# The second DFT stage of k*v by halves of the channels, in threes of frequencies

## The chip, the cores and the metric

The kernel runs on one core of one Trainium2 chip. The metric is the device time of one execution in microseconds. Five engines work side by side, each with its own queue, in order: TensorE (PE, with its weight loads PEld), VectorE (DVE), ScalarE (ACT), GpSimd (POOL) and SyncE (SP), whose queue issues most transfers. TensorE writes its results to PSUM; ScalarE or VectorE copies ("evicts") them to SBUF.

## What is computed

One block with two parts, over x = A_q of 2048 positions and 640 channels, in bf16, with six modulation vectors made of a condition c. What matters here, cut from the reference:

```python
mod = (_silu(c) @ w_mod).reshape(c.shape[0], 6, 1, -1)       # sa, ca, ga, sb, cb, gb
h = _layernorm(x) * (1 + ca) + sa
# part A: short convolution of k (4 taps) times v, then a long convolution over all positions
kv = k_shift * v
kv_f = rfft(pad(kv), over positions); kf_f = rfft(pad(ssm_k))
y = irfft(kv_f * kf_f)[:S] + kv * ssm_D
x = x + ga * (h * y)
# part B: two gelu MLPs with layer norms, the first with shifts between four channel groups
h = _layernorm(x) * (1 + cb) + sb
h1 = _gelu(_layernorm(h) @ w1); hs = shifted(h1) @ w2; x1 = h + hs
x = x + gb * (x1 + _gelu(_layernorm(x1) @ w3) @ w4)
```

## The kernel before, in words

**The long convolution** is a DFT of 4096 points split into two factors, done with matmuls. Channels lie on partitions in 5 blocks (`ND`); `to_slots` (L392) transposes 32 x 32 pieces on VectorE. `stage1` (L400) multiplies by a small DFT matrix, per channel block b and half h of the channels, and its evictions fill `T01`: the half h = 0 goes to `T0`, h = 1 to `T1`. `stage2` (L417) goes over the 32 frequencies k: for each it does four matmuls (two row halves of the array, g, times two terms, cc), each over the 320 columns of both halves of the channels, into one PSUM slot, and one eviction of 640 elements per partition (`evac`, L206: ScalarE at L209, VectorE at L211). It is called twice: for ssm_k into `KSX` (region R3), and for k*v into `XS` (region R5).

The inverse starts with `inverse1` (L603), ten times, i = 5 h + b. Step i reads block i of `XS`, 2048 columns that hold all 32 frequencies of a tenth of the channels: VectorE multiplies it by the spectrum `kx` and by a copy `ky` of the spectrum with the partition halves swapped (L613, two products per step, into a ring of two pairs `TAB` in Rb). The copy comes by two transfers (L609, one on SP's queue and one on POOL's) into a ring of four buffers `KSY`, which are pieces of RG, RK and Rb: the piece of RK also holds a modulation weight and the small table `Ht`, the piece of Rb the last block of k*v. TensorE then does 2 x 16 matmuls (L624, L625), and two evictions of 1024 elements go to `Zh[h]`, which is `T0` or `T1` again. `inverse2` (L653, matmuls at L665) ends the convolution in groups of two or three position tiles.

**Around it.** `mods` makes the modulation vectors in twelve halves: a weight load from w_mod on SP (L484), five matmuls (L490), an eviction into `modv`. `ln1_stats` and `make_q` make the first normalisation and modulation of each position tile A. `chain_a`, `chain_b`, `chain_c` gate, add, normalise and transpose each tile; `mm_w1`, `mm_w2`, `mm_w3`, `mm_w4` (matmuls L822 and L832, L877, L911, L941) are part B. w3 and w4 are loaded into `T01` once `inverse2` has read all of it.

**What sets the order.** The functions only add tasks to a `Planner`, with dependencies between the regions that they read and write, and with costs and rates that some search outside the kernel used. `run` (L122) takes the order written out in `ORDER`: a number for the task, a letter for its engine (P TensorE, A ScalarE, D VectorE, G POOL, S SP), and after a colon the PSUM slots, of which there are four of two banks each. Each engine executes its tasks in that order. Costs, rates and `port` are not read by `run`.

Of the kernel before, what the change touches and what calls it, by code (L numbers as in the profile page):

```python
# [15 lines left out]
S, D, F = 2048, 640, 1728  # L16
# [10 lines left out]
19G 18D 2S 27G 21G 20D 29D 30A 50G 23D 28D 31A 22D 25A 36G 24A 37G 0S 68G 26G 69D 90P:0 91A 86P:1 84P:2 87A 4S 85A 72G 52D 3S 70G 73D 106P:3 107A 6S  # L27
49G 102P:0 104P:1 105A 71D 96P:2 97A 88P:3 103D 5S 74D 75D 8S 118P:0 98P:1 9S 119D 1S 66D 38G 39G 40A 89A 99A 114P:2 115D 108P:3 92P:0 93A 109A 116P:1
10S 112P:2 94P:0 122P:3 67D 32G 41G 42G 43G 51D 44A 45D 117D 54A 53A 95A 113A 80P:0 81A 11S 123D 110P:1 111D 76P:2 77A 7S 100P:3 101D 82P:0 83A 78P:1
136D 34S 33G 120P:2 121D 46G 55G 79A 179P:3 180A 47S 185P:0 186A 35S 141P:1 142A 191P:3 192D 147P:0 148A 201S 143P:2 144D 175P:1 176A 171P:3 172D  # L30
137P:0 138A 183P:2 184A 195P:1 196D 145P:3 146A 169P:0 170D 48S 163P:2 164A 149P:1 193P:3 194A 197P:0 150D 198D 161P:2 162A 12S 56G 173P:1 174A 204S
189P:3 190D 57G 58G 157P:0 153P:2 154D 151P:1 202S 177P:3 158A 178D 59G 152A 165P:0 166A 139P:2 140D 203S 13S 155P:1 156A 187P:3 188D 159P:0 160A
181P:2 182A 60A 254D 14S 167P:1 168D 199P:3 200D 260P:0 261A 124P:2 212A 268P:0 269A 266P:1 267A 211D 126P:3 125D 127D 262P:0 214D 209A 270P:2 271A
263A 128P:1 264P:3 265A 130P:2 215A 255D 276P:0 15S 129D 61G 210D 65G 258P:3 259A 277A 62G 16S 134P:1 280P:3 281A 131D 63G 17S 135D 363G 278P:2 279A
64A 274P:0 275A 132P:1 213G 272P:3 273A 362S 220S 221P:2 222A 256D 288P:0 289A 133D 257D 282P:1 223S 224P:3 225A 226S 286P:2 287D 283A 284P:0 285D
229S 292P:3 293A 232S 294P:1 295A 290P:2 291D 296P:3 297A 227P:0 228D 387G 230P:1 348P:2 322P:3 239S 231D 480A 235S 349A 340P:0 341A 233P:1 251G 323D
242S 250G 234D 326P:2 360P:3 361D 327A 356P:0 357A 328P:1 329D 241S 358P:2 359A 306P:3 336P:0 337D 307A 314P:1 315A 318P:2 319D 248S 238G 354P:3 355A
320P:0 321D 310P:1 311A 483D 300P:2 252S 330P:3 244S 331D 301A 352P:0 353A 236P:1 253G 237D 308P:2 309A 205S 245G 316P:3 317D 324P:0 325A 350P:1 351D
312P:2 313A 249G 247S 332P:3 333A 243S 246G 298P:0 299D 304P:1 305A 344P:2 345D 302P:3 303A 386S 240G 371G 338P:0 342P:1 343A 339D 334P:2 346P:3 347A
370S 335D 364D 365D 368P:0 369A 366P:1 367A 378S 481D 379G 372D 373D 374P:2 375A 376P:3 377A 486D 487D 380D 381D 442S 443P:0 388D 389D 394S 382P:1  # L40
383A 384P:2 396D 385A 217A 395G 392P:3 397D 402S 403G 390P:1 404D 405D 410S 391A 398P:2 393A 411G 400P:1 412D 399A 408P:3 418S 409A 406P:2 407A 401A
413D 414P:3 415A 416P:2 419G 421D 417A 420D 424P:1 422P:3 425A 423A 448S 449P:2 489A 427G 426S 428D 450A 429D 430P:1 431A 432P:3 434S 435G 437D 433A
436D 438P:2 439A 440P:1 441A 454S 490D 457S 444D 458P:0 479G 445S 455P:3 484D 485D 491D 488D 495P:21 218D 459A 482D 451S 216G 456A 492D 493D 496D 494D
497A 519D 452P:0 453A 446P:3 447D 219G 501G 520D 522G 540D 521A 560D 541D 475S 511P:12 524D 561D 472S 478G 513A 532A 533D 553D 523G 498P:03 499A 500A
591D 588D 525D 534D 527D 592D 542A 589D 512A 543G 545D 544G 563G 565D 502P:20 504A 562A 564G 526A 477S 528G 529D 503A 594D 566D 590A 546D 505P:31 476S
507A 593A 595G 530P:0 531A 567A 568D 547A 548D 651D 600D 601D 508P:21 509A 506A 596D 510A 535P:0 536A 549G 550D 602D 603A 551P:2 206S 569G 570D 597D
537P:3 538A 552D 598D 599A 652D 604D 605G 571P:1 208S 572D 554D 555D 558P:0 559A 606D 609D 473S 654D 655D 556P:2 557A 578P:3 579A 474S 576P:1 577A
610P:0 611D 207S 464D 607P:2 608D 514S 653A 657G 656A 658G 580P:3 581D 582A 620P:1 621A 659D 618P:0 619A 663D 664D 583G 584G 665D 585D 660D 666A
586P:2 625P:3 661D 662A 518G 587A 636P:1 637A 515S 638P:0 639A 622P:2 667D 668G 669D 640P:1 463A 670S 626D 627A 671D 672S 681P:3 517S 679P:0 623D 624A
628D 629G 633D 682A 630D 573D 641A 634P:2 635D 460D 631P:3 642P:1 632D 574D 680A 683P:2 684D 686P:0 687D 643A 575D 703P:1 461A 699P:3 719D 720D 465G  # L50
462G 615D 467A 612D 613D 616D 704A 697P:2 688A 689G 614D 685A 690G 691D 692P:0 700A 694A 695P:1 721A 693D 701P:3 702A 696D 769P:0 765P:1 516S 698A
617D 785D 786D 787A 722D 723D 644P:3 725G 673D 674D 675D 788D 789D 724A 790A 726G 727D 731A 763P:2 770A 791G 466D 728D 729D 730A 645D 792G 705P:03
764A 767P:2 706P 732D 733D 734A 468G 766A 735D 736G 793D 794D 797D 798D 799D 800A 795D 796A 741D 739D 707D 740S 737A 738S 749P:1 750A 747P:0 801G 802G
646D 648S 748A 803D 805D 804S 806S 815P:1 816A 676D 677D 678D 713D 714D 851D 852D 853A 742D 743D 708D 710S 712S 813P:3 711S 754P:0 751P:1 814A 817P:3
709S 854D 855D 856A 755D 752D 768A 771P:02 820P:1 857G 858G 859A 647S 860D 861D 863D 864D 715S 757G 772P 865D 867D 756A 753A 758G 761D 862A 762S 818D
821D 823D 866A 759A 760S 835P:3 819A 822A 868G 869A 824G 827A 871D 773D 470A 872S 836A 825D 779D 780D 829P:1 870S 875P:0 650S 828S 876A 469A 471G 807D
744D 873P:2 745D 826S 895P:3 833P:0 874A 877P:2 896A 808D 809D 834A 914D 880P:3 716S 891P:0 878D 830A 881D 882A 915D 649S 774D 892A 879A 893P:1 831P:2
889P:3 810A 811D 781S 812D 883G 884G 885A 887D 832A 837P:02 894A 886S 888S 955P:1 717S 746D 911D 912D 890A 913A 971D 972D 916A 917G 918G 839D 923D
953P:3 919D 920D 921D 778S 777S 924D 718S 925D 927D 974G 973A 975G 976A 977D 978D 980G 922A 926A 928G 838P 954A 845D 956A 979A 775S 929D 930S 840D
949P:0 897P:23 931A 932S 935P:1 936A 981G 898P 982D 950A 983S 986P:1 987A 783S 539G 841S 933P:0 984P:1 842S 899D 776S 846D 850S 782S 847S 905D 934A  # L60
940P:2 937P:3 941D 985A 848S 938D 844S 784S 900D 989P:0 843S 906D 907S 988G 1023P:1 1024D 951P:2 943G 1026D 992P:3 904S 942A 939A 944G 945D 952A 947D
948S 957P:12 901S 990D 991A 946S 1007P:0 1025A 1027G 993D 1003P:3 994A 995D 996G 997D 1028A 1029S 959D 910S 1008A 999A 998S 1004A 1058P:1 1001P:0
1002A 1005P:3 1000S 1036P:0 1006A 958P 1037A 1032P:3 1033A 1034P:0 1035A 1030P:3 1031A 849S 965D 1062D 960D 961S 908S 903S 902S 966D 969S 1009P:20
964S 1052P:3 909S 1010P 1053A 1011D 1054P:2 1012D 1015S 1055A 1017D 962S 1038P:30 1016S 967S 963S 1018D 970S 1022S 1020S 1021S 1056P:2 1057A 968S
1040D 1041D 1042S 1045S 1043S 1014S 1039P 1046D 1013S 1047D 1044S 1019S 1049S 1050S 1063D 1059A 1051S 1060P:32 1061P 1064D 1065D 1068S 1069S 1066S
1048S 1070D 1071D 1067S 1072S 1074S 1073A 1075A
# [72 lines left out]
def kernel(  # L139
# [294 lines left out]

    def dep(t, *on):
        for o in on:
            if o not in t.deps:
                t.deps.add(o)
                o.succ.append(t)
# [42 lines left out]
    def mod_half(i, j, hf):  # L482
        w, wk = wm[i % 3] if i < EARLY else wl[i - EARLY]
        dma("SP", 410, lambda q: q.dma_start(w, mod_d[:, :, j * D + 320 * hf:j * D + 320 * hf + 320]), w=[wk], rate=250.0)  # L484
# [96 lines left out]
    stage2(XS, "R5")  # L581
# [21 lines left out]
    def inverse1(h, b):  # L603
# [4 lines left out]
        for o in range(2):  # L608
            dma("SP" if o == 0 else "POOL", 256, lambda q, o=o: q.dma_start(ky[64 * o:64 * o + 64, :], kx[64 - 64 * o:128 - 64 * o, :]), r=[kxk], w=[kk + ("y",)], rate=235.0)  # L609
# [90 lines left out]
    def ln_finish(li, t0, n, quick):  # L700
# [4 lines left out]
        def f(e):  # L705
# [3 lines left out]
            else:  # L709
                eng_of[e].tensor_tensor(rs, nm, nm, ALU.mult)  # L710
                eng_of[e].tensor_scalar(rs, rs, -1.0, EPS, ALU.mult, ALU.add)
        add(("POOL", "DVE"), {"POOL": 0.33 * (1 + n), "DVE": 0.15 + 0.12 * n}, f, r=[("s1", 100 * li + t0, 100 * li + t0 + n)], w=[("nm" + k, 0, 1)])

        def f(e):
            if n == 1:
# [353 lines left out]
```

## Time and profile before

| what | value |
|---|---|
| median of 4 runs | 307.48 us (306.92 to 307.85) |
| profiled execution, whole | 307.59 us |
| its span, first to last instruction | 305.8 us |
| busy PE, DVE, ACT, POOL | 272.7, 222.4, 207.2, 112.4 us |
| mean granted TensorE clock | 0.957 |
| first and last L426 matmul of the second call of `stage2` | 62.1 and 74.3 us |
| first L613 product, last L613 product (starts) | 75.36 and 98.22 us |
| first L665 matmul | 102.8 us |
| first L911 matmul | 141.24 us |
| last L932 matmul | 300.20 us |

In the rows of the profile L12 is line 12 of the kernel before. A row of a group gives the line, engine and operation, output<-input by the program's names, partitions x elements, the number of instructions, and then busy us, mean ns of one, and idle time of the engine just before, with what ended it. A row in order of time gives start, duration, engine, line, and in brackets the idle time before it. A row of stretches gives the busy us of each engine between two times. Instructions that follow each other on one engine overlap a little, so that n of them in a row take less than n means. POOL in the chain and DMA rows are transfers by name of their buffers.

### The profile page before, as it was taken

The numbers are of one execution on the slowest core, as the hardware profiler recorded it, in microseconds if no ns is written. First come the engines' busy times: TensorE is split into PE (matmuls) and PEld (weight loads), VectorE is DVE, ScalarE is ACT, GpSimd is POOL, SyncE is SP. The second block draws the span as 40 slices with busy tenths as digits, with TensorE's granted clock in tenths as the row PEclk, the third lists the DMA queues.
The fourth block names the chain that finished last, engine by engine and source line by source line (L and its number), as shares of the span: only waits on it lengthen the run. The fifth ranks groups of instructions, "written<-read, shape, count | busy, mean of one in ns | idle before, by whom it ended". The sixth has DMA issues, their size and how long they took to land.

```text
span 305.8 us, 7408 instructions
## 1 busy us (share of the span) xinstructions
PE 272.7 (89%) x2922; PEld 207.3 (68%) x2926; DVE 222.4 (73%) x437; ACT 207.2 (68%) x355; POOL 112.4 (37%) x257
## 2 busy tenths in 40 slices
PE   0998999997899946697999999999999999999993
PEld 0655655754888724686788777688877777987761
DVE  8999999999999998885688996835755355031343
ACT  4779999998589669986986648875854535522110
POOL 4798066051122786342454722312434042000000
PEclk9999999999799965789999999999999999999998
DMA  5999999779799950961100041250112213201112
GB/s 170 258 204 203 208 198 248 207 197 241 201 230 299 265 104 7 356 212 25 42 3 1 2 91 32 46 107 2 34 37 44 61 29 73 58 11 29 47 39 52
DMA packets 58146, 35.73 MB, mean 117 GB/s; under 512 B 39872, under 2 KB 54848, under 8 KB 58112
## 3 DMA queue, kind: packets, MB, share of 16 engines
q1 hardware_dynamic: 56864, 31.68, 43.2%
q0 software_dynamic: 1152, 3.54, 4.5%
q8 instruction: 23, 0.38, 0.5%
q14 instruction: 11, 0.09, 0.1%
q10 hardware_dynamic: 96, 0.04, 0.1%
HBM read 16.31 MB, written 2.62 MB: 62 GB/s over the span
## 4 chain that ended last, share of the span: by engine, by line
PE 56%; ACT 15%; DVE 10%; DMA 7%; issue 5%; POOL 5%; SPq 0%; ACTq 0%; DVEq 0%; POOLq 0%
PE ps_w L911 20%; PE ps_w L941 19%; PE ps_w L877 6%; ACT T L209 4%; DVE Rb L613 4%; ACT R L209 4%; PE ps_w L822 3%; DMA Ra<-in_A_ssm_k_dram 2%; ACT RG L733 2%; PE ps_s L426 2%; DMA RK<-R 2%; ACT Rb L209 2%; PE ps_s L409 1%; DMA Rb<-R 1%; POOL R L310 1%
## 5 line engine op out<-in xcount | busy, mean ns | idle before, releaser
L911 PE MATMUL ps_w<-R,T 128*128 128x256 bf16 (+1 forms) x630 | 64.3, 261 | 1.0 <-ACT R L782 1.0
L911 PEld LDWEIGHTS <-T 128*128 128x128 bf16 x630 | 55.7, 98 | 8.7 <-issue 2.6
L941 PE MATMUL ps_w<-T,R 128*128 128x320 bf16 x416 | 59.1, 299 | 0.0
L915 ACT ACTIVATE R<-ps_w 128x1024 bf16<-128x1024 f32 (+2 forms) x36 | 29.4, 831 | 36.2 <-PE ps_w L911 30.3
L941 PEld LDWEIGHTS <-R 128*128 128x128 bf16 x416 | 40.5, 98 | 15.2
L964 DVE TENSOR_TENSOR T<-ps_w,R 128x640 bf16<-128x640 f32 x15 | 12.3, 823 | 32.0 <-PE ps_w L941 18.8
L209 ACT CAST T<-ps_s 128x1024 bf16<-128x1024 f32 x33 | 31.4, 1018 | 3.0 <-PE ps_s L409 3.0
L409 PE MATMUL ps_s<-F1bd,Rb 128*128 128x256 bf16 x160 | 22.6, 293 | 9.5 <-DVE Rb L396 8.3
L733 ACT ACTIVATE RG<-R 128x640 bf16<-128x640 bf16 x32 | 23.5, 734 | 10.0 <-DVE R L884 6.5
L409 PEld LDWEIGHTS <-Rb 128*128 128x128 bf16 x160 | 16.6, 105 | 15.6 <-DVE Rb L396 8.3
L209 ACT CAST R<-ps_s 128x640 bf16<-128x640 f32 x37 | 23.4, 721 | 1.2 <-PE ps_s L426 1.2
L624 PE MATMUL ps_i<-EA,Rb 128*128 128x128 bf16 x160 | 20.8, 229 | 2.8 <-DVE Rb L613 2.4
L877 PE MATMUL ps_w<-RG,R 128*128 128x320 bf16 x160 | 23.2, 299 | 0.0
L209 ACT CAST T<-ps_i 128x1024 bf16<-128x1024 f32 x20 | 19.0, 1025 | 5.9 <-PE ps_i L625 5.8
L426 PE MATMUL ps_s<-T,RG 64*128 64x320 bf16 x256 | 22.2, 297 | 0.5 <-DMA RG<-RG 0.2
L625 PE MATMUL ps_i<-EB,Rb 128*128 128x128 bf16 x160 | 20.6, 229 | 1.6 <-DVE Rb L613 1.5
L822 PE MATMUL ps_w<-R,RG 128*128 128x256 bf16 (+1 forms) x200 | 21.8, 276 | 0.0
L719 POOL TENSOR_TENSOR lnv<-lnv,mhalf 128x2 f32<-128x2 f32 (+1 forms) x29 | 20.9, 720 | 2.3
L211 DVE CAST R<-ps_s 128x640 bf16<-128x640 f32 x27 | 20.7, 818 | 0.9 <-PE ps_s L426 0.3
L838 ACT ACTIVATE R<-ps_w1x 32x256 bf16<-32x256 f32 (+1 forms) x40 | 13.2, 331 | 10.6 <-PE ps_w1x L832 10.2
L822 PEld LDWEIGHTS <-RG 128*128 128x128 bf16 x200 | 19.0, 111 | 1.6 <-issue 0.2
L884 DVE SCALAR_TENSOR_TENSOR R<-ps_w,R 128x640 bf16<-128x640 f32 x16 | 13.1, 821 | 9.0 <-PE ps_w L877 9.0
(176 smaller groups left out, 510.0 us busy)
## 6 DMA issues: line engine op xcount, KB each, us to landing
Ra<-in_A_ssm_k_dram SPq DMA_DIRECT2D x5, 512.0 KB, 6.5
Ra<-in_A_q_dram SPq DMA_DIRECT2D x8, 320.0 KB, 6.1
R<-in_w_mod_dram SPq DMA_DIRECT2D x6, 400.0 KB, 7.3
out_dram<-RH SPq DMA_DIRECT2D x60, 40.0 KB, 1.6
T<-in_B_w_dram SPq DMA_DIRECT2D x1, 2160.0 KB, 9.6
T<-in_B_w_dram SPq DMA_DIRECT2D x1, 2080.0 KB, 14.7
RH<-in_w_mod_dram SPq DMA_DIRECT2D x4, 400.0 KB, 5.0
RK<-R SPq DMA_DIRECT2D x5, 256.0 KB, 4.8
```

The source lines that it names most:

```text
L209: nc.scalar.copy(dst, src(ps.tile))
L211: nc.vector.tensor_copy(dst, src(ps.tile))
L409: nc.tensor.matmul(psv[:, ml, :], lhsT=xL[:, s0:s0 + P], rhs=F1r, start=True, stop=True)
L426: nc.tensor.matmul(psv[:, g], lhsT=Gs[p, k, 64 - 64 * cc:192 - 64 * cc], rhs=T1b[p, cc * 32 + k], start=(cc == 0), stop=(cc == 1), tile_po ...
L624: nc.tensor.matmul(psv[:, w, :], lhsT=Av[:, r_, :, g_], rhs=EAf, start=True, stop=False)
L719: nc.gpsimd.tensor_tensor(rs, rs, mhalf[:, 0:n], ALU.pow)
L733: add("ACT", 0.74, lambda e: nc.scalar.activation(junk, src, ACT.Square, scale=float(D) ** -0.5, accum_out=stat[:, li, 1, t:t + 1]), r=[sk ...
L822: nc.tensor.matmul(pt[:, fb, 0:cw], lhsT=w1_sb[:, b, 160 * fb:160 * fb + P], rhs=hT[:, b, 0:cw], start=(b == 0), stop=(b == ND - 1))
L877: nc.tensor.matmul(pt[:, hf, 0:320], lhsT=gsf[:, fb, c0:c0 + P], rhs=w2_sb[:, fb, 320 * hf:320 * hf + 320], start=(fb == 0), stop=(fb == 4))
L911: nc.tensor.matmul(pt[:, fl, 0:cw], lhsT=w3_sb[:, b, fb * P:(fb + 1) * P], rhs=xT[:, b, 0:cw], start=(b == 0), stop=(b == ND - 1))
L915: nc.scalar.activation(g3[g % 2][:, f0:f0 + fn, 0:cw], ps.tile[:, 0:fn, 0:cw], ACT.Gelu_apprx_tanh)
L941: nc.tensor.matmul(bank(i, hf), lhsT=gg[:, fb, i * P:(i + 1) * P], rhs=w4_sb[:, fb, 320 * hf:320 * hf + 320], start=(fb == 0 and i == 0), ...
```

## The change

`stage2(XS, "R5")` is replaced by two calls of a new function, one per half of the channels. Each goes over the frequencies in threes (ten of three and one of two): per group 24 (or 16) matmuls of 160 columns, and one eviction of 960 (or 640) elements. A half reads its half of `T01` and writes its half of `XS`. The first call of `stage2`, for ssm_k, stays. The order is written anew from the first word to the last, so that tasks also change place and engine elsewhere; numbers of tasks from 298 on are shifted. Some costs and rates differ. The whole program has 256 more rows on TensorE (128 weight loads and 128 matmuls), 12 fewer on VectorE, 3 more on ScalarE, 6 fewer on POOL, as many on SP.

```diff
+    def stage2_half(h):
+        for k0 in range(0, 32, 3):
+            kn = min(3, 32 - k0)
+            ps = Slot()
+
+            def f(e, ps=ps, k0=k0, kn=kn):
+                psv = pst(ps, name="ps_s2")[:, :, 0:480].rearrange("p g (k s) -> p g k s", k=3)
+                for j in range(kn):
+                    k = k0 + j
+                    for cc in range(2):
+                        for g in range(2):
+                            p = slice(64 * g, 64 * g + 64)
+                            nc.tensor.matmul(psv[:, g, j], lhsT=Gs[p, k, 64 - 64 * cc:192 - 64 * cc], rhs=T1h[h][p, cc * 32 + k],
+                                             start=(cc == 0), stop=(cc == 1), tile_position=(64 * g, 0))
+            t0 = add("PE", 0.17 * kn, f, r=[("T01", 10240 * h, 10240 * h + 10240), ("RG", 192 * k0, 192 * (k0 + kn))], alloc=ps, ni=8 * kn)
+            w = [("R5", 10240 * h, 10240 * h + 10240, "s2"), ("kT", 4 * h, 5, "s2")] + ([("vT", 0, 5, "s2")] if h else [("kTp", 0, 1, "s2")])
+            t1 = evac(XS[:, 160 * h:160 * h + 160, k0:k0 + kn, :],
+                      lambda t, kn=kn: t[:, :, 0:480].rearrange("p g (k s) -> p s k g", k=3)[:, :, 0:kn], 320 * kn, ps, w)
+            dep(t1, t0)
...
-    stage2(XS, "R5")
+    for h in range(2):
+        stage2_half(h)
...
-        dma("SP", 410, lambda q: q.dma_start(w, mod_d[:, :, j * D + 320 * hf:j * D + 320 * hf + 320]), w=[wk], rate=250.0)
+        dma("SP", 410, lambda q: q.dma_start(w, mod_d[:, :, j * D + 320 * hf:j * D + 320 * hf + 320]), w=[wk], rate=340.0)
...
-        add("POOL", 1.1 if quick else 1.5, f, r=[("s2", 100 * li + t0, 100 * li + t0 + n), ("nm" + k, 0, 1)], w=[("ln" + k, 0, 1)])
+        add("POOL", 0.8 if quick else 1.1, f, port=-1, r=[("s2", 100 * li + t0, 100 * li + t0 + n), ("nm" + k, 0, 1)], w=[("ln" + k, 0, 1)])
```

What the new order does, by engine:

| | before | after |
|---|---|---|
| evictions of the k*v second stage, ScalarE | 19 of 640 | 15 of 960, 1 of 640 |
| the same, VectorE | 13 of 640 | 5 of 960, 1 of 640 |
| evictions of the ssm_k second stage, ScalarE and VectorE | 18 and 14 | 20 and 12 |
| evictions of stage 1 for ssm_k, ScalarE and VectorE | 16 and 4 | 17 and 3 |
| evictions of `inverse1`, ScalarE and VectorE | 20 and 0 | 19 and 1 |
| `ln1_stats`, ScalarE and VectorE | 9 and 7 | 7 and 9 |

On VectorE the last eviction of the first half is followed by one multiplication of q, three products, the one eviction of the second half that VectorE does, and the other seventeen products in a row. On ScalarE six evictions of the second half come first, then the other four between the evictions of `inverse1`. One stage-1 eviction of k*v (its matmuls too) stands within the first half. Of the modulation weights, the sine on ScalarE that frees RK for the third load comes before six more stage-1 evictions of k*v than it did; on SP the load of w1 comes before five of the last six w_mod loads. The last group of `inverse2` comes behind the first three matmul groups of `mm_w1`. Of the first 30 us: the addition of ssm_D for channel block 4 goes from VectorE to POOL, behind the mask of `RQ` (L357), and the sign flip of the first `Gs` block (L350) stays on POOL, but behind the rounding steps of the second.

```diff
-229S 292P:3 293A 232S 294P:1 295A 290P:2 291D 296P:3 297A 227P:0 228D 387G 230P:1 348P:2 322P:3 239S 231D 480A 235S 349A 340P:0 341A 233P:1 251G 323D
-242S 250G 234D 326P:2 360P:3 361D 327A 356P:0 357A 328P:1 329D 241S 358P:2 359A 306P:3 336P:0 337D 307A 314P:1 315A 318P:2 319D 248S 238G 354P:3 355A
...
+290P:0 291A 469D 288P:1 289A 233P:3 234D 292P:2 293A 294P:0 296P:3 230P:1 297A 298P:2 295D 299A 466D 342S 253G 246S 248G 312P:0 308P:3 309A 231D 463D
+300P:1 301A 313D 460D 251G 310P:2 311D 367G 243S 306P:0 307A 316P:3 317D 280P:1 281A 252G 314P:2 304P:0 302P:3 305A 249S 240G 315D 236P:1 303A 237D
+318P:2 319D 467D 340P:0 345D 241S 341A 338P:1 339A 238S 242G 326P:3 327A 344D 245S 250G 366S 322P:2 334P:0 352D 330P:1 331D 323A 244G 335A 239G 247G
...
```

## The prediction

> **What bounds the kernel now.** I read the busy time of each engine by stretches first, then VectorE's and ScalarE's instructions in order of time, then the groups, then the chain. The stretches (busy us, count of instructions; granted TensorE clock, DMA share, GB/s at the end):
>
> ```profile
> core 0: us, PE busy (x) PEld busy (x) DVE busy (x) ACT busy (x) POOL busy (x), PEclk, DMA share, GB/s
> 62.00:75.40 13.40, 12.49 (x140) 7.18 (x138) 12.03 (x19) 12.78 (x20) 5.00 (x10) 1.00 0.94 228
> 75.40:103.00 27.60, 24.06 (x369) 21.72 (x373) 27.50 (x33) 21.70 (x28) 8.25 (x16) 0.94 0.92 253
> 103.00:141.20 38.20, 25.99 (x672) 20.50 (x652) 33.19 (x88) 31.32 (x68) 21.33 (x53) 0.73 0.54 159
> 141.20:160.00 18.80, 18.25 (x200) 15.71 (x200) 12.86 (x34) 15.72 (x34) 8.25 (x22) 1.00 0.13 27
> 160.00:200.00 40.00, 39.61 (x320) 30.06 (x319) 33.93 (x85) 27.21 (x52) 16.96 (x45) 1.00 0.17 36
> 200.00:300.50 100.50, 100.43 (x872) 79.18 (x870) 42.89 (x95) 45.37 (x80) 18.07 (x57) 1.00 0.20 44
> ```
>
> From 141.2 to 300.5 TensorE idles 1.0 us of 159.3: it sets the time there, and an earlier start of that stretch is an earlier end. Before it, from 75.4 to 103, VectorE is busy 27.5 of 27.6 us: the products of the inverse transform. ScalarE is not:
>
> ```profile
> 70.52 4.66 DVE L211 CAST R<-ps_s 128x640 bf16<-128x640 f32 x6 [0.16 <-PE ps_s L426]
> 75.36 1.23 DVE L613 TENSOR_TENSOR Rb<-R,R 128x2048 bf16<-128x2048 bf16 x1 [0.18 <-ACT R L209]
> ...
> 98.22 1.22 DVE L613 TENSOR_TENSOR Rb<-R,R 128x2048 bf16<-128x2048 bf16 x1
> ```
>
> ```profile
> 70.25 5.08 ACT L209 CAST R<-ps_s 128x640 bf16<-128x640 f32 x8 [0.22 <-PE ps_s L426]
> 79.47 1.01 ACT L209 CAST T<-ps_i 128x1024 bf16<-128x1024 f32 x1 [4.15 <-PE ps_i L625]
> ...
> 91.47 6.53 ACT L209 CAST T<-ps_i 128x1024 bf16<-128x1024 f32 x7 [0.52 <-PE ps_i L625]
> ```
>
> Both engines evict the second stage until 75.3; no product can start before the last eviction; then ScalarE waits 4.15 us while VectorE makes the first products. The sizes that I work with:
>
> ```profile
> L426 PE MATMUL ps_s<-T,RG 64*128 64x320 bf16 x256 | 22.2, 297 | 0.5 <-DMA RG<-RG 0.2 <-ACT R L209 0.2
> L209 ACT CAST R<-ps_s 128x640 bf16<-128x640 f32 x37 | 23.4, 721 | 1.2 <-PE ps_s L426 1.2
> L211 DVE CAST R<-ps_s 128x640 bf16<-128x640 f32 x27 | 20.7, 818 | 0.9 <-PE ps_s L426 0.3
> L209 ACT CAST Rb<-ps_i 128x960 bf16<-128x960 f32 x7 | 6.5, 953 | 2.8 <-PE ps_i L665 2.8
> ```
>
> The chain of waits passes through one copy of the kernel's spectrum that comes late, and ends in the stretch of TensorE:
>
> ```profile
> 69.86 6.29 DMA RK<-R
> ...
> 141.24 2.39 PE ps_w L911 x40
> ```
>
> **The evictions.** In a row one costs less than its mean, because neighbours overlap: 5.08/8 = 0.635 us on ScalarE and 4.66/6 = 0.777 on VectorE for 640 elements, 6.53/7 = 0.933 on ScalarE for 1024. For 960 I take 0.88 on ScalarE (0.635 plus the difference of the means, 953 - 721, gives 0.87; on the line to 1024 it is 0.88) and 1.11 on VectorE (the 1024 form has a mean of 1219 against 818; 320/384 of that on top of 0.777). Before: 19 on ScalarE and 13 on VectorE, 12.1 + 10.1 = 22.2 us. After: ScalarE has 15 of three frequencies and one of two, 15 x 0.88 + 0.64 = 13.8; VectorE five and one, 5 x 1.11 + 0.78 = 6.3. VectorE loses 3.8 us, ScalarE gains 1.7. That the access pattern gets one more dimension I cost at nothing: the 960 form of the later inverse step has as many, and fits the line.
>
> **The matmuls.** 128 of 320 columns become 256 of 160, with as many more weight loads. In the trace the four of one frequency start at 65.62, 65.64, 65.75 and 65.77: two row halves of the array run side by side, 0.135 us per pair of 320 columns. Pairs of 160 columns at half of that: 64 half-frequencies x 2 pairs x 0.068 = 8.7 us. If the pairs did not overlap at all, the inverse products give the other end: their 128-column matmuls, each with its own weights, start 0.055 apart (85.17, 85.23, 85.28), so 160 columns cost 0.069 and 256 of them 17.7 us. The Trainium skill has a rule against this change (TensorE: Matmul & The Clock Gate, section Back-to-back issue gap): in a stream of weight loads and matmuls the spacing is about 81 ns at 128 columns and 131 at 512, so short matmuls lose; by it 160 columns are an estimated 0.085 and the stage 21.8 us. The trace has 0.055 where the rule has 0.081, so I take the row, and within its ends 10 us, because this very line shows the pairs side by side. Then TensorE stays under ScalarE's 13.8. By the rule the second half of the channels would be ready some 2.7 us later than I have it below.
>
> **Up to the last inverse step (L665, first start 102.8).** ScalarE from its first eviction of the stage: 13.8, one stage-1 eviction that now stands behind it 0.93, 19 inverse evictions (one goes to VectorE) x 0.933 = 17.7, the statistics of tile 6, 1.6 (86.52 to 88.13 before): 34.0 us. I add 1.5 us of idling where the first inverse evictions wait for products; before it is 5.8 in this stretch. From 62.4 this ends at 97.9.
> VectorE, checked apart: from 62.9 to 104.17 it works 41.3 us before. Less: evictions 3.8, statistics of tile 7 to ScalarE 1.1, two scalings (0.36) and two multiplications (0.41) of q earlier or later 1.5. More: one inverse eviction 1.16. Net -5.2. The 20 products, 1.136 apart, are untouched; ten of them now lie beside ScalarE's evictions of the second half. Both engines say the same: the last inverse step starts near 98, 4.8 us earlier. The tenth product ends near 62.4 + 6.3 (first half evicted) + 11.4 + 1.5 = 81.6, and the last eviction of the second half, behind ten of these and five inverse evictions on ScalarE, at about the same time; neither gates the other by more than 1 us.
>
> **Who waits for the copies.** The copy that gated the chain at 76.15 needs the buffer of a modulation weight and the sixteen small copies out of RK. The third weight load stood until 54.88 behind ScalarE's last sine (54.33); that sine moves some 6 us up, and the first five modulation matmuls stand ahead of the stage. The copy can be issued at about 68 (ten POOL issues of 0.5 us first), lands at 73 to 74, and its product is due at 73.7: nothing, at most 0.5 us. On SP the 800 KB of w1 now pass ahead of five modulation loads: some 3.0 MB from about 85 on, at the 205 to 304 GB/s of that time 10 to 14.5 us, so landed at 95 to 99.5. Their four matmuls (2.7 us, two of them stood ahead before) come right behind the first last-step group, and the second and third groups, and their evictions, queue behind them on TensorE: nothing to 1.5 us; I take 0.3.
>
> **The first 62 us.** ScalarE takes over one eviction of stage 1 and two of the first second stage (+0.93, +1.27; VectorE -1.16, -1.55); it gives back the scaling of a q tile (0.82) and the late eviction (0.93). The addition for the fourth channel block of ssm_k goes from VectorE to POOL behind a 2.47 us mask, so its transpose starts near 15.9 instead of 14.1, 1.8 us in which VectorE waits, against 2.7 us that it loses. The sign flip at L350 (1.51 us on POOL from 15.63) moves behind three more POOL steps (0.76, 1.94, 1.29) and ends near 21.5, where its transfer was issued at 20.88: up to 1 us later. Ends -1 and +1.5; I take +0.3, which is the 62.4 above.
>
> **Normalisation, 103 to 141.2, and after.** The planner's numbers (rate, port, costs) are read by nothing that runs: only the written order acts. VectorE's instructions up to the first w2 sum are 27.4 us before and 26.8 after by the same rows; so 38.2 us stays, between -2 and +3. The w3 load needs the last group of L665, which now stands behind three w1 matmul groups: issued near 118.5, 9.6 us, against a first use near 136. That cover of 8 us was 10 before. In TensorE's stretch no work is added; VectorE gets 2.5 us more (three statistics, two eviction-like pieces, less scalings) where it has 6.1 free between 160 and 200. Its gain can be 1.0 at most; I take 0.
>
> Sum: 305.8 - 4.8 + 0.3 = 301.3 for the span. The profiled execution took 307.59, 1.8 around the span, and is 0.1 above the median of 307.48: 303.0.
>
> **Rivals.**
> *The bound moves within the stage.* TensorE at the rule's spacing, or ScalarE with 20% more for the three-frequency pattern (16 x 0.18 = 2.8), delays the second half's products by 2.7. For: nothing in the trace runs 160 columns in 64-row pairs. Against: the 0.055. Time: 303.0 + 2.7 = 305.7; with late modulation loads too, 307, no change.
> *The pieces fit better.* The idling of 1.5 falls away and the normalisation loses 2: 299.5.
> *TensorE starves behind the gain (slower).* The order of the last two thirds is new as well, and a stretch with 1.0 us of idling can only get worse. If VectorE's 2.5 us and its three added pieces fall in front of the w2 and normalised tiles between 150 and 200, each delay is TensorE's whole. For: VectorE is 33.93 of 40 there. Against: 6.1 us free, and ScalarE 12.8. From 4.5 us of starving it is no gain; five tile pairs waiting 1.3 each give 6.5: 309.5.
> *The change does not do what it says:* products could stay behind all evictions. The built order excludes that: three products stand before VectorE's only eviction of the second half, and ScalarE does the other ten beside the products.
>
> **How the numbers follow.** Forecast 0.55, better fit 0.08, moved bound 0.18, starving 0.19. A measurement tells 0.2% (0.6 us). The first two are faster; of the moved bound 0.13 is faster, 0.05 the same; starving is slower: 0.76, 0.05, 0.19. The forecast's own range is 300.5 to 305.3; leaving a tenth on each side over all cases gives 298 to 309.3.
>
> **What would show it.** Right: VectorE's first product near 69 with second-half evictions on ScalarE beside it; ScalarE's idling between 75 and 100 under 2.5 us; L665 first near 98; first L911 near 136.5; idling of TensorE from there about 1 us. Wrong: L426 spaced over 0.05 us with ScalarE waiting for it; 960-element evictions over 1.0 apart; L490 waiting behind L665; over 4 us idling of TensorE behind the first L911.

## The result and the profile after

The kernel after takes 306.56 us (median of 37 runs, 304.08 to 310.83) against 307.27 before (58 runs): ratio 0.9963, 95% interval 0.9949 to 0.9976. It is 0.4% faster. The forecast was 303.0, 1.5% faster; the time lies inside its range of 298.0 to 309.3, outside the likeliest case's 300.5 to 305.3.

The profiled execution has a span of 305.12 us, 0.64 less than before. Line numbers are now those of the kernel after: L446 is the matmul of the new function, L633 the product, L685 the last inverse step, L842 and L852 w1, L897 w2, L931 w3, L961 and L952 w4, L796 the transposes on TensorE, L208 and L210 the evictions, L608 and L610 the scaling of a q tile, L562 and L563 the statistics on ScalarE.

| mark (us) | before | after | difference |
|---|---|---|---|
| first k*v second-stage matmul | 62.14 | 62.78 | +0.6 |
| first product | 75.36 | 70.71 | -4.7 |
| first last-inverse matmul | 102.83 | 97.80 | -5.0 |
| first w3 matmul | 141.24 | 138.06 | -3.2 |
| last L952 (L932 before) matmul | 300.20 | 300.09 | -0.1 |
| span | 305.76 | 305.12 | -0.6 |

So the front part gained what was forecast, and the gain was given back in two places: 1.9 us between the first last-inverse matmul and the first w3, and 3.1 us behind it. The stretches of the kernel after, cut at these marks (busy us and instructions of PE, PEld, DVE, ACT, POOL; granted clock, DMA share, GB/s):

```profile
core 0: us, PE busy (x) PEld busy (x) DVE busy (x) ACT busy (x) POOL busy (x), PEclk, DMA share, GB/s
62.00:70.70 8.70, 8.46 (x181) 6.86 (x180) 8.30 (x12) 8.34 (x11) 5.41 (x11) 1.00 0.80 201
70.70:97.80 27.10, 24.74 (x429) 22.12 (x424) 26.99 (x28) 26.77 (x33) 6.88 (x11) 1.00 0.93 241
97.80:138.06 40.26, 28.50 (x693) 21.83 (x693) 34.85 (x89) 35.69 (x77) 23.09 (x52) 0.79 0.47 135
138.06:160.00 21.94, 20.29 (x220) 17.61 (x218) 16.86 (x47) 15.75 (x30) 8.03 (x27) 1.00 0.40 118
160.00:200.00 40.00, 38.69 (x313) 29.29 (x312) 31.27 (x81) 26.23 (x53) 17.07 (x40) 1.00 0.20 33
200.00:300.50 100.50, 98.41 (x851) 76.86 (x849) 41.62 (x92) 44.03 (x76) 15.96 (x51) 1.00 0.22 45
```

In the second row ScalarE now works 26.77 of 27.10 us, VectorE 26.99: the 5.8 us in which ScalarE waited are filled. In the last three rows TensorE idles 1.65 + 1.31 + 2.09 = 5.05 us, where it idled 1.0 before.

VectorE of the kernel after in order of time: three evictions of 960 elements in a row take 3.27 us, 1.09 each; three products stand before its one eviction of the second half.

```profile
65.50 3.27 DVE L210 CAST R<-ps_s 128x960 bf16<-128x960 f32 x3
...
70.71 1.22 DVE L633 TENSOR_TENSOR Rb<-R,RG 128x2048 bf16<-128x2048 bf16 x1
71.84 2.36 DVE L633 TENSOR_TENSOR Rb<-R,R 128x2048 bf16<-128x2048 bf16 x2
74.12 1.15 DVE L210 CAST R<-ps_s 128x960 bf16<-128x960 f32 x1
...
93.51 1.22 DVE L633 TENSOR_TENSOR Rb<-R,RK 128x2048 bf16<-128x2048 bf16 x1
```

ScalarE beside it: four of 960 elements in 3.56 us, 0.89 each, and second-half evictions between those of the inverse until 82.9.

```profile
63.41 3.56 ACT L208 CAST R<-ps_s 128x960 bf16<-128x960 f32 x4
...
80.00 2.08 ACT L208 CAST T<-ps_i 128x1024 bf16<-128x1024 f32 x2
81.80 1.14 ACT L208 CAST R<-ps_s 128x960 bf16<-128x960 f32 x1
```

The group of the new matmuls (name, shapes, count, busy us, mean ns, idle before):

```profile
L446 PE MATMUL ps_s<-T,RG 64*128 64x160 bf16 x256 | 10.6, 230 | 0.5 <-ACT R L208 0.3 <-DVE R L210 0.2
```

256 matmuls of 160 columns keep TensorE busy for 10.6 us, and it waits 0.5 us for evictions. In a row their pairs start at 66.932, 67.001, 67.070: 0.069 us a pair.

What TensorE waits for from the first w3 on (us in total, times, longest), first before, then after:

```profile
PE ps_w L911 <- ACT R L782: 1.0, 1, 1.0
PE ps_w1x L832 <- DVE lnv L711: 0.5, 1, 0.5
PE ps_w1x L832 <- DMA R<-RK: 0.4, 1, 0.4
```

```profile
PE ps_w1x L852 <- DMA R<-RK: 2.2, 2, 1.2
PE ps_w L931 <- DMA R<-RH: 1.9, 2, 1.4
PE ps_w L931 <- ACT Rb L208: 0.5, 1, 0.5
PE ps_w L842 <- DMA R<-RK: 0.3, 1, 0.3
```

Five waits, 4.4 us in sum where there were 0.4, are for tiles that a DMA transposes (into R from RK for w1, from RH for w3). The matmul groups stand on TensorE's queue before their tiles are there. Counted from the first w3, the tiles of the first two of these waits land no later than before the change (5.2 and 38.1 us, against 5.2 and 39.3): there it is the place on TensorE's queue. Those of the other three land 3.7, 7.3 and 3.8 us later (46.3, 71.4 and 120.1 us, against 42.6, 64.1 and 116.3): there the engines that make them come to them later as well.

The first w3 matmul is not the same point of the work in both orders. Before, one w2 group of ten matmuls stands just ahead of it, and the next behind its first 40 matmuls:

```profile
138.76 1.52 PE L877 MATMUL ps_w<-RG,R 128*128 128x320 bf16 x10
141.24 2.39 PE L911 MATMUL ps_w<-R,T 128*128 128x128 bf16 x40 [0.95 <-ACT R L782]
143.47 1.52 PE L877 MATMUL ps_w<-RG,R 128*128 128x320 bf16 x10
```

After, both w2 groups stand ahead of it:

```profile
135.34 2.88 PE L897 MATMUL ps_w<-RG,R 128*128 128x320 bf16 x20
138.06 1.28 PE L931 MATMUL ps_w<-R,T 128*128 128x128 bf16 x20
```

The tile that w3 reads is evicted at 141.19 before (L782), and w3 starts at once; in the kernel after it is evicted at 137.25 (L804), 0.8 us ahead of w3. So of the 1.9 us, 0.8 are the second w2 group ahead of the mark, and 1.1 are a tile that comes later. Behind the mark TensorE has ten matmuls less to do in the kernel after: what it loses there, counted at equal work, is its idling, 4.0 us.

### The profile page after: what moved, and what is told of

Same layout as the page of the kernel before. It is cut to its first block, busy times and chain, and to the rows that moved or that the text cites. A ratio compares the mean times of both kernels' runs of the same rounds, so it can differ in the third digit from the quotient of the medians.

```text
span 305.1 us, 7648 instructions
## 1 busy us (share of the span) xinstructions
PE 270.6 (89%) x3050; PEld 207.3 (68%) x3054; DVE 218.0 (71%) x432; ACT 210.2 (69%) x352; POOL 113.0 (37%) x251
## 4 chain that ended last, share of the span: by engine, by line
PE 59%; DVE 15%; POOL 7%; DMA 6%; ACT 5%; issue 5%; SPq 1%; DVEq 0%; POOLq 0%; ACTq 0%
PE ps_w L931 17%; PE ps_w L961 15%; PE ps_s L408 5%; PE ps_ksh L480 5%; PE ps_w L897 4%; PE ps_w L842 3%; DVE Rb L633 3%; ACT R L208 2%; POOL lnv L739 2%; DMA R<-RH 2%; PE ps_i L644 2%; PE ps_i L645 2%; DMA R<-RK 2%; DMA RH<-in_w_mod_dram 2%; DVE R L780 1%
## 5 line engine op out<-in xcount | busy, mean ns | idle before, releaser
L931 PE MATMUL ps_w<-R,T 128*128 128x256 bf16 (+1 forms) x630 | 64.6, 261 | 2.4 <-DMA R<-RH 1.9
L931 PEld LDWEIGHTS <-T 128*128 128x128 bf16 x630 | 55.6, 98 | 10.0 <-issue 3.9
L935 ACT ACTIVATE R<-ps_w 128x1024 bf16<-128x1024 f32 (+2 forms) x36 | 29.0, 829 | 48.4 <-PE ps_w L931 48.2
L961 PE MATMUL ps_w<-T,R 128*128 128x320 bf16 x416 | 59.0, 299 | 0.0
L961 PEld LDWEIGHTS <-R 128*128 128x128 bf16 x416 | 40.2, 98 | 15.6 <-issue 0.5
L208 ACT CAST T<-ps_s 128x1024 bf16<-128x1024 f32 x34 | 32.9, 1021 | 3.8 <-PE ps_s L408 3.8
L208 ACT CAST R<-ps_s 128x640 bf16<-128x640 f32 (+1 forms) x36 | 27.5, 845 | 1.0 <-PE ps_s L425 0.6
L739 POOL TENSOR_TENSOR lnv<-lnv,mhalf 128x2 f32<-128x2 f32 (+1 forms) x29 | 23.6, 814 | 2.3
L897 PE MATMUL ps_w<-RG,R 128*128 128x320 bf16 x160 | 23.9, 303 | 0.0
L842 PE MATMUL ps_w<-R,RG 128*128 128x256 bf16 (+1 forms) x200 | 21.0, 267 | 0.9 <-ACT Rb L208 0.5
L726 POOL TENSOR_SCALAR lnv<-stat 128x2 f32<-128x2 f32 (+1 forms) x14 | 4.9, 349 | 45.2 <-DVE Ra L764 18.1
L644 PE MATMUL ps_i<-EA,Rb 128*128 128x128 bf16 x160 | 19.1, 219 | 1.2 <-ACT T L208 0.5
L842 PEld LDWEIGHTS <-RG 128*128 128x128 bf16 x200 | 17.9, 106 | 3.2 <-issue 1.6
L897 PEld LDWEIGHTS <-R 128*128 128x128 bf16 x160 | 15.6, 99 | 6.3 <-issue 0.5
L645 PE MATMUL ps_i<-EB,Rb 128*128 128x128 bf16 x160 | 19.0, 219 | 0.5 <-DVE Rb L633 0.5
L738 POOL TENSOR_TENSOR lnv<-stat,lnv 128x2 f32<-128x2 f32 x19 | 4.0, 212 | 40.1 <-ACT RG L753 26.6
L208 ACT CAST T<-ps_i 128x1024 bf16<-128x1024 f32 x19 | 18.5, 1124 | 0.3 <-PE ps_i L645 0.3
```

The lines of the kernel that those rows point to most:

```text
L208: nc.scalar.copy(dst, src(ps.tile))
L644: nc.tensor.matmul(psv[:, w, :], lhsT=Av[:, r_, :, g_], rhs=EAf, start=True, stop=False)
L645: nc.tensor.matmul(psv[:, w, :], lhsT=Bv[:, r_, :, g_], rhs=EBf, start=False, stop=True)
L739: nc.gpsimd.tensor_tensor(rs, rs, mhalf[:, 0:n], ALU.pow)
L842: nc.tensor.matmul(pt[:, fb, 0:cw], lhsT=w1_sb[:, b, 160 * fb:160 * fb + P], rhs=hT[:, b, 0:cw], start=(b == 0), stop=(b == ND - 1))
L897: nc.tensor.matmul(pt[:, hf, 0:320], lhsT=gsf[:, fb, c0:c0 + P], rhs=w2_sb[:, fb, 320 * hf:320 * hf + 320], start=(fb == 0), stop=(fb == 4))
```

## The experiments

Two theories. **O**, the order: the newly written order of the last two thirds places matmul groups ahead of their tiles, and the gain is lost there. **N**, the normalisation cannot go faster, whatever its order. Later two more: **F**, TensorE's program arrives late behind bulk loads; **W**, work of ScalarE was moved behind the gain.

Executions with the same front differ by up to 2.4 us in their arrival at the second stage (61.9 to 64.3 us: a load of v or of a modulation weight lands earlier or later). So stretches are compared, not clock times (g1 is read by its time alone):

| kernel | second stage to last inverse | to first w3 | from there to last L952 | ratio to before |
|---|---|---|---|---|
| before | 40.7 | 38.4 | 159.0 | 1 |
| after | 35.0 | 40.3 | 162.0 | 0.9963 |
| e2b: old front, new rest | 40.7 | 38.9 | 161.0 | 1.0109 |
| e1b: new front, old rest | 34.8 | 42.4 | 158.9 | 0.9935 |
| e3b: threes, no overlap | 40.7 | 39.1 | 162.5 | 1.0132 |
| e4b: five places changed | 34.9 | 39.1 | 173.5 | 1.0339 |
| f1: new order to w3, then old | 34.8 | 42.4 | 159.0 | 0.9922 |
| f2: after, loads held | 35.7 | 40.3 | 161.0 | 0.9928 |
| f3: f1, loads held | 35.4 | 40.6 | 159.0 | 0.9925 |
| f4: e1b, loads held | 35.7 | 39.0 | 158.8 | 0.9853 |
| g2: f4, scalings on VectorE | 35.0 | 40.5 | 159.5 | 0.9868 |
| g3: after, scalings left out | 34.9 | 38.8 | 161.0 | 0.9928 |
| g4: before, loads held | 40.7 | 37.9 | 158.8 | 0.9958 |

**The first four: spoilt by the PSUM slots.** These hybrids had the slots (the digits behind the colon) dealt out anew, to the slot freed first in the text, for the whole program, also where the order is that of the kernel after:

```diff
-118P:0 ... 94P:1 ... 116P:1 ... 80P:3
+118P:1 ... 94P:0 ... 116P:3 ... 80P:2
```

> The kernel after, with its new order kept up to the first group of the last inverse step (so the threes, the two halves and the early products stay) and from there on the order of the kernel before. Theory O (the gain of 5.0 us at the first last inverse step is lost because the newly written order of the rest puts matmul groups on TensorE ahead of tiles that are not there yet): first last inverse step still near 97.8, first w3 matmul near 136.3, idling of TensorE after it near 2.5 us as before, time about 302.5, ratio to before about 0.984. Theory N (the normalisation and what it waits for cannot go faster whatever the order; the work moved out of the front has to be done there): first last inverse step near 97.8, but first w3 near 138 or later, time 305.5 to 306.5, ratio 0.995 to 0.998.

> The reverse: the kernel before up to the first group of its last inverse step (one second stage over all channels, products behind all evictions), and from there on the order of the kernel after. Theory O: first last inverse step near 102.8, then the new order's losses of 1.8 us up to w3 and 3.1 us in TensorE's stretch: time about 312, ratio 1.013 to 1.018. Theory N: the rest takes what it took before: 307 to 308, ratio 0.998 to 1.003.

> The kernel after with all evictions of the second half ahead of the first product, shared between ScalarE and VectorE, so that the threes stay and the overlap is gone; the rest of the order as in the kernel after. If the overlap is what brings the last inverse step forward: first product near 74.5 instead of 70.7, first last inverse step 101 to 102, all later marks 3.5 us later and the time 309.5 to 310.5 by theory O (ratio 1.007 to 1.011); by theory N, where the rest is not limited by this start, about 307. If the threes alone bring it: first last inverse step near 98.5, time about 307.

> The kernel after with only five places of TensorE's order in its last stretch changed: two w1 groups whose transposed tiles come by DMA late are put behind one w3 or w2 group each, and two w4 groups that are ready are put ahead of a w1 or w3 group that waits; one eviction on ScalarE follows its w4 group. Theory O: the waits of TensorE for DMA transposes (2.2 us ahead of w1, 1.9 us ahead of w3) fall to under 1.5 in sum, time 303.5 to 304.5, ratio 0.988 to 0.992. Theory N: the waits come back at the next tile, time 306 to 307, ratio 0.995 to 0.999.

Measured: 311.89 us (1.0127, 1.0096 to 1.0159), 314.14 (1.0199, 1.0169 to 1.0229), 314.48 (1.0214, 1.0184 to 1.0245) and 322.74 (1.0499, 1.045 to 1.0547). All miss, and say nothing on the theories: e1 and e4 have the front order of the kernel after word for word, and take 39.3 us from the second stage to the last inverse step instead of 35.0. All four were repeated with the slots kept.

**e1b and e2b: which part loses?** e1b keeps the new order up to the first group of the last inverse step (task 475 and its evictions), and then has the words of the old one, slots included; e2b is the reverse.

```diff
 475P:20 477D 476A
-520D 459G 454S 499D 500D 471D 521D 472A 540D 434S 219G 523D 541D
...
+459G 471D 472A 434S 437S 438P:1 439A 435P:3 428S 429P:2 430A 431S
...
```

> The same question as in the run with the old rest, but with every word of the new order's front (PSUM slots included) as in the kernel after, and the slots of the rest as in the kernel before, since the earlier hybrids had their slots dealt out anew and were late from 28 us on. Theory O (the new order of the rest loses the 5.0 us): first last inverse step 97.8, first w3 near 136.5, time 302.5 to 303.5, ratio 0.984 to 0.988. Theory N (the rest can't go faster whatever its order): first last inverse step 97.8, first w3 at 138 or later, time 305.5 to 307, ratio 0.995 to 1.0.

> The reverse with the slots of each part as they were: front of the kernel before, rest of the kernel after. Theory O: first last inverse step 102.8, time 310.5 to 312, ratio 1.011 to 1.016. Theory N: 307 to 308, ratio 1.0 to 1.003.

e1b: 305.64 us, 0.9935 (0.9908 to 0.9962); e2b: 311.22, 1.0109 (1.0049 to 1.017). The third column of the table decides half of it for O: TensorE's stretch takes 158.9 us with the old order behind the new front, 161.0 with the new order behind the old front. The waits of e2b, where nothing came early, show the same places:

```profile
PE ps_w1x L832 <- DMA R<-RK: 2.2, 2, 1.1
PE ps_w L911 <- DMA R<-RH: 1.2, 1, 1.2
PE ps_w L822 <- DMA R<-RK: 0.3, 1, 0.3
```

The other half went against O: the old order needed 42.4 us from the last inverse step to w3. TensorE of e1b, in order of time (start, us, what; idle before and what ended it), shows where:

```profile
103.55 1.87 PE L685 MATMUL ps_i<-T,RH 32*32 32x160 bf16 x127 [0.76 <-issue]
106.46 0.22 PE L685 MATMUL ps_i<-T,RH 32*32 32x160 bf16 x1 [1.04 <-ACT Rb L208]
111.67 0.60 PE L685 MATMUL ps_i<-T,RH 32*32 32x160 bf16 x33 [4.98 <-issue]
```

It stood still for 4.98 us in the middle of a group, with nothing that releases it.

**e3b: is it the overlap or the threes?** The eleven evictions of the second half stand ahead of the first product, in turn on both engines.

```diff
-340P:0 345D 241S 341A 338P:1 339A 238S 242G 326P:3 327A 344D
+340P:0 341A 338P:1 339D 326P:3 327A 322P:2 323D 334P:0 335A 330P:1 331D
+324P:3 325A 320P:2 321D 328P:0 329A 332P:1 333D 336P:3 337A 345D 241S
```

> The kernel after with its slots, only the eleven evictions of the second half put ahead of the first product, in turn on ScalarE and VectorE: threes without overlap. If the overlap is worth what the forecast's VectorE account says (five evictions of 1.09 us back on VectorE, products later by 3.8 to 5.5): first product 74.5 to 76, first last inverse step 101.5 to 103, time 309.5 to 311.5 by theory O, 306.5 to 308 by theory N. If the threes alone bring the gain: first last inverse step under 99.5.

311.96 us, 1.0132 (1.0074 to 1.019). From the second stage to the last inverse step it takes 40.7 us, as before the change: the 5.7 us are the overlap, with the evictions that it lets ScalarE take from VectorE; larger evictions alone gave nothing that can be seen.

**e4b: mending TensorE's order by hand.** Two w1 groups that wait go behind one group each; two w4 groups go ahead of one that waits. Three slots (of tasks 869, 871 and 875) change with it.

```diff
-661P:3 619A 662A 659P:2 660A 622P:1
+619A 622P:1 661P:3 662A 659P:2 660A
...
-875P:0
+817P:30 875P:1
```

> The kernel after with five places of TensorE's order in its last stretch changed as in the earlier run, but with the slots kept (six slots change hands in the whole order). Theory O: same as the kernel after up to 160 us, TensorE's waits for transposes by DMA fall from 4.4 us to under 2, time 303.5 to 305, ratio 0.988 to 0.993. Theory N: 306 to 307.

317.45 us, 1.0339 (1.0258 to 1.0421): both theories missed. The waits did not fall: L931 for a DMA transpose 3.3 us, L931 for ScalarE's gelu (L935) 3.2, L897 for L844 2.5. So moving TensorE's groups alone does not mend the order: that the order from w3 on costs the time rests on e1b, e2b and f1, and which of its places costs how much stays open.

**f1: the old order from the first w3 on.**

```diff
 604A
-620P:2 621A 495S 616P:1 617A 618P:0 661P:3 619A
+616P:1 617A 495S 618P:0 619A 620P:1 661P:3 659P:0
...
```

> The new order as it stands up to the first w3 matmul group, and from there the order and slots of the kernel before. From the runs so far: TensorE's stretch lasts 162.0 us in the new order (161.0 behind the old front), 158.9 in the old one (also behind the new front). If that stretch is lost by its order alone: first w3 still near 138.0, idling of TensorE behind it near 2.5 us, span 302, time 303.0 to 304.0, ratio 0.987 to 0.990. If the stretch depends on what the normalisation leaves behind (which tiles are how far), the idling comes back: time 305.5 to 306.5.

305.32 us, 0.9922 (0.9894 to 0.995). TensorE's stretch is 159.0 with 2.5 us of idling, as O has it, and its waits for DMA transposes fall from 4.4 us to 0.9. The time is 1.3 us above what O expected, and in the profiled execution w3 began at 139.47, not 138: two modulation weights landed late (L509 waited 4.3 us for them), and at the join TensorE waits 1.2 us for an eviction on ScalarE (L208) before the first w3, whose tile had been there since 136.8.

**f2, f3, f4: theory F.** The packets of TensorE's program are in the trace: 16 KB each, on a queue of their own (q8). In three kernels one lands at 111.46 (before), 108.53 (after) and 110.42 (e1b), and TensorE goes on at 112.70, 109.82 and 111.67, 1.24 to 1.29 us behind it. In e1b none starts between 100.65 and 109.19. The DMA queues of e1b from 100.70 to 109.10 (packets, MB, share of the 16 engines):

```profile
q1 hardware_dynamic: 1545, 1.83, 104.4%
q14 instruction: 1, 0.01, 0.6%
```

The engines are full with w2 (640 KB), loads of x (320 KB each) and modulation weights, of which w2 is not used before 128 us. So w2 and the loads of x were held until POOL has come to a given point:

```diff
+    def late(t, old):
+        def g(e):
+            old(e)
+            nc.gpsimd.memset(RG[:, 3200:3201], 0.0)
+        t.fn = g
+    late(pl.tasks[544], pl.tasks[544].fn)
...
-544G 507D
+544G 453S 455S 208S 207S 206S 507D
```

In f4 the point is task 503, and all four loads of x are held.

> The kernel after, with the 640 KB and 40 KB of w2 and three loads of x (320 KB each) moved on SP's queue behind a point near 108.5 us (a memset of one column of w2's place on POOL holds them), so that no bulk load is under way from about 103 to 108.5. Theory F (the last inverse step's matmuls stand still without a releaser, 1.9 us in the kernel after, because the next 16 KB of TensorE's program land behind the bulk loads): the wait of L685 without a releaser falls under 0.7, the first transpose comes at 111.5 to 112.5 instead of 113.4, first w3 near 136.5, time 305 (ratio 0.991 to 0.994). Theory C (the normalisation is bound by its chain of VectorE, ScalarE and POOL): first transpose within 0.4 of 113.4, first w3 near 138, time 306 to 307.

> Both edits: the joined order, and the loads of w2 and x held to 108.5 us. Theory F: 1.5 us below the joined order alone, time 301.5 to 302.5, ratio 0.982 to 0.985. Theory C: as the joined order, within 0.4 us.

> The new front with the old order of the rest (305.6 us, 0.9935), where L685 stood still for 5.0 us without a releaser, with the same loads held to about 107.5 us. Theory F: that wait falls under 1.5 us, first transpose 113 to 114 instead of 117.2, first w3 near 136.5, time 302 to 303, ratio 0.982 to 0.986. Theory C: the wait shifts to another engine, first transpose stays at 116 or later, time 305 to 306.

f2: 305.13 us, 0.9928 (0.9901 to 0.9955); f3: 305.0, 0.9925 (0.9905 to 0.9945); f4: 302.27, 0.9853 (0.9825 to 0.988). The same stretch of f4's queues, 100.7 to 109.1:

```profile
q1 hardware_dynamic: 1001, 0.62, 23.9%
q8 instruction: 2, 0.03, 1.3%
```

Two pieces of program arrive where none did, and the standstill of L685 falls from 7.1 us in sum to 1.2 (e1b to f4, 97 to 118 us) and from 1.9 to nothing (after to f2). The mechanism of F is shown. What it was worth is another matter: the old order behind the new front gained 3.4 us in the stretch to w3, f2 nothing. There the wait only changed its name (f2, TensorE, 97 to 118 us):

```profile
PE ps_tr L796 <- DVE RK L748: 4.5, 2, 4.3
PE ps_i L685 <- ACT Rb L208: 1.8, 1, 1.8
PE ps_i L685 <- ACT modv L524: 0.8, 1, 0.8
```

The first transpose comes at 113.19 with the loads held and 113.36 without: the tile's own chain on ScalarE, POOL and VectorE sets it. For the 1.9 us of the kernel after, F is not the cause. The time of f2 is in F's range by luck: its gain is not where F had it, and its interval overlaps that of the kernel after. f3 misses F's forecast, and is what theory C had. The Trainium skill (Runtime: NRT & Kernel Launch, section Instruction fetch mechanics) has the program come in 16 KiB blocks with a cost that is mostly hidden; the size agrees, but it is not hidden here: 1.9 to 5.0 us in one wait while the DMA engines are full.

**g4: does it belong to the change?** The same hold in the kernel before, behind its step at 111.7.

```diff
-523G
+523G 473S 475S 206S 208S 207S
```

> The kernel before with three of its loads of x and the main loads of w2 held behind POOL's step near 111.7 us. If held loads help any order in which a 16 KB piece of TensorE's program is asked for during them: TensorE's wait without a releaser at 110.2 (2.1 us) falls under 0.7 and the time by 1 to 2 us: 305.5 to 306.5, ratio 0.993 to 0.997. If what they give belongs to the early start alone: 307.0 to 307.8, ratio 0.998 to 1.001.

306.96 us, 0.9958 (0.9933 to 0.9983). TensorE's standstill of L665 (3.5 us in two before) is gone, and the time is 0.4% shorter: that much of f4's gain is to be had without the change, the rest (0.9853 against 0.9958) is not.

**g1, g2, g3: theory W.** ScalarE between the last inverse step and the first w3, by groups, before:

```profile
L588 ACT ACTIVATE RQ<-Ra,nb,rs 128x640 bf16<-128x640 bf16 x1 | 0.9, 920 | 0.0
```

and after:

```profile
L608 ACT ACTIVATE RQ<-Ra,nb,rs 128x640 bf16<-128x640 bf16 x4 | 3.7, 923 | 0.0
L562 ACT ACTIVATE RQ<-Ra 128x640 bf16<-128x640 bf16 x1 | 0.7, 739 | 0.0
L563 ACT ACTIVATE RQ<-Ra 128x640 bf16<-128x640 bf16 x1 | 0.7, 737 | 0.0
```

Four scalings of q tiles instead of one, and the statistics of tile 7: ScalarE's busy time in this stretch rises from 31.5 to 35.7 us, VectorE's from 33.4 to 34.9. g1 gives the four scalings to VectorE, g2 does so in f4 (with the statistics), g3 keeps the order and cuts these operations to one column, so that q of tiles 4 to 7 and the statistics of tile 7 are left out.

```diff
-472A ... 512A ... 553A ... 533A
+472D ... 512D ... 553D ... 533D
```

```diff
+            if A == 7:
+                jk, xa = jk[:, 0:1], xa[:, 0:1]
             nc.scalar.activation(jk, xa, ACT.Identity, scale=1.0 / D, accum_out=mv1[:, A, 0:1])
...
+                m = 1 if small else 640
+                nc.scalar.activation(dst[:, 0:m], src[:, 0:m], ACT.Identity, scale=sc, bias=bi)
```

> The kernel after with the scalings of the q tiles 4 to 7 (four of 0.92 us on ScalarE, all behind the first group of the last inverse step or beside it) given to VectorE (0.44 each) at the same places of the order. Theory W (the 1.9 us are ScalarE's deferred work): first last inverse step to first w3 39.3 or less instead of 40.3, time 305.0 to 305.8. Theory C (the chain through POOL's square roots and the tile's steps sets it): 40.0 to 40.6, time 306.3 to 306.9.

> New front, old order of the rest and held loads (302.3 us, 0.985), with the three scalings of q tiles and one tile's statistics that ScalarE does there given to VectorE, as in the kernel before. Theory W: 0.5 to 1 us less, 301.3 to 301.8. Theory C: no difference, or up to 0.5 more where VectorE is the later engine: 302.2 to 302.8.

> The kernel after with ScalarE's scalings of the q tiles 4 to 7 and its statistics of tile 7 cut to one column each (so these parts of q are left unscaled, and the statistics of tile 7 are of one column): some 4.2 us of ScalarE's work less at the same places, every wait kept. Theory W: first last inverse step to first w3 38.4 to 39.0, first w3 near 136.5, time 305.0 or less (TensorE's stretch as in the kernel after). Theory C: 39.8 or more, time 306 to 306.6.

g1: 307.2 us, 0.9974 (0.9949 to 0.9999); g2: 304.15, 0.9868 (0.9827 to 0.9908); g3: 305.91, 0.9928 (0.9894 to 0.9962). g3's stretch to w3 is 38.8 us with 32.8 of ScalarE's work, as W has it, though its time is 0.9 above what W expected; g1 and g2 bring nothing. But e4b speaks against W. Up to the first w3 it has the order and the slots of the kernel after, with all of ScalarE's work (36.0 us busy), and its tile for w3 is evicted 37.9 us behind the first last-inverse matmul: as in g3 without that work (38.0), and no later than in the kernel before (38.4). In the kernel after it is 39.5. The two executions are level 28.2 us behind that matmul. From there TensorE does the same w1 and w2 matmuls more slowly in the kernel after:

```profile
125.97 1.98 PE L842 MATMUL ps_w<-R,RG 128*128 128x128 bf16 x20 [0.55 <-ACT Rb L208]
128.81 2.00 PE L897 MATMUL ps_w<-RG,R 128*128 128x320 bf16 x10
```

than in e4b:

```profile
125.04 1.28 PE L842 MATMUL ps_w<-R,RG 128*128 128x128 bf16 x20 [0.54 <-ACT Rb L208]
127.15 1.53 PE L897 MATMUL ps_w<-RG,R 128*128 128x320 bf16 x10
```

The rows of these 4 us, first after, then e4b, differ in the granted clock (the third number from the end):

```profile
125.80:129.80 4.00, 3.83 (x34) 3.45 (x34) 2.93 (x7) 3.34 (x10) 0.68 (x4) 0.57 1.02 410
124.89:128.89 4.00, 3.50 (x40) 2.66 (x40) 3.01 (x8) 3.91 (x12) 1.02 (x5) 1.00 1.01 408
```

f2 has the same dip of the clock (tile at 39.5), g3 and e2b do not (38.0 and 37.7). So of the 1.9 us up to w3, 0.8 are the place of a w2 group, and 1.1 go with a low clock in the profiled execution; nothing is left that ScalarE's moved work has to explain. The kernel before has such a dip too (0.50 from 125.8 to 132.6), and g4, which has the old order and held loads, has none there (tile at 37.9): without the dip both orders take the same in these executions. What sets it, and how many executions have it, no run here shows.

**A version that beats both** is f4: the new front, the old order of the rest, and the loads held: 0.9853 of the time before.

## Why the prediction was wrong

*Right, within 0.5 us.* Evictions of 960 elements: 0.88 and 1.11 expected, 0.89 and 1.09 found. Matmul pairs 0.068 expected, 0.069 found; the stage's 10 us were 10.6. The row was the right choice against the rule with 21.8 us: TensorE waited for the evictions, not they for it. The copy landed at 72.64 and 73.65 (73 to 74 expected). The first 62 us cost 0.6 instead of 0.3, within what executions differ. The last inverse step began at 97.80 (near 98), and e3b shows that the overlap brought it. That ScalarE's sum came out to 0.1 us is in part luck: its first eviction of the stage stands at 63.41, not 62.4, and it idles 0.5 us, not 1.5.

*Off, with little effect.* The modulation loads landed between 95.99 and 102.10, not by 99.5. The w3 load was issued at 122.27, not near 118.5.

*Off in size: "38.2 us stays".* By the marks it was 40.3. Of the 1.9 us, 0.8 are the second w2 group ahead of the first w3, which the step did not count; 1.1 go with the low granted clock, of which the working says nothing, though its row for this stretch shows 0.73. The step counted VectorE's instructions alone (27.4 to 26.8) and left out ScalarE, to which the change gives 4.2 us more in this stretch. That hole cost nothing that the runs show: e4b does the same work, and its tile for w3 is there after 37.9 us, against 38.4 before.

*Failed: "I take 0" for TensorE's stretch.* It was 3.1 us (162.03 against 158.96) with ten matmuls less to do, and 4.0 us by TensorE's idling: the prediction's own sign of being wrong, over 4 us of idling behind the first w3 (5.05), came. It shows in every kernel of the table whose order from w3 on is the new one as written (161.0 to 162.5 in five), and in none with the old one (158.8 to 159.5 in seven); TensorE idles 3.9 to 5.3 us there in the five, 0.9 to 2.5 in the seven. The rival of starving behind the gain had the right mechanism in its general form, an order that leaves a full engine waiting, and the wrong place and size: not VectorE's added 2.5 us, but five groups queued up to 1.4 us ahead of a DMA transpose, and some 4 us where it put 4.5 to 6.5. "No work is added" was true and beside the point: an engine with 1.0 us of idling is full only as long as every tile comes in its queue's order.

In sum: -5.03 up to the last inverse step, +1.1 until w3's tile is there, +3.8 from there to the last L952 (0.8 of it ahead of the first w3), and -0.53 behind that (5.03 to the end instead of 5.56): -0.64 us of span.

## What to carry to other kernels

A mark compares two orders only where the same work lies ahead of it, so look at what stands just before and just behind it in both. Before a difference of 1 us between single executions is given a cause, compare two executions of one order (here the kernel after and e4b), with the granted clock of each. Where a queue is in order and its engine idles under 1%, a new order is a cost of its own, to be read tile by tile (when is each operand there, when is its matmul up) and not set to nothing because no instruction is added. A hybrid of two orders, with the slots of each part kept, tells in two runs which half of a change loses.

## What was not expected of the hardware

The pieces of TensorE's program (16 KB) queue with the data: with the DMA engines at 104% of their share none started for 8.5 us, and TensorE stood for 4.98 us. Moving 680 KB of w2 and the loads of x by some 8 to 13 us, still ahead of their first use, gave 0.4% in the kernel before and 0.8% behind the new front with the old order.

Which PSUM slot a group gets, with each engine's order unchanged, lengthened the way from the second stage to the last inverse step from 35.0 to 39.3 us (e1 and e4), and the time by 2.5 to 6.3 us between the four first hybrids and their repetitions.

TensorE's granted clock dips in one execution and not in another, with the same instructions in the same order up to there: 0.57 against 1.00 over 4 us. The 20 w1 matmuls took 1.98 us instead of 1.28, and w3's tile came 1.6 us later.
